# A fused attention, MLP and Fourier block on one core: TensorE's attention work grouped by two units, and two copies moved to other engines

## The chip, the cores and the metric

One core of a Trainium2 chip runs the whole program. The metric is the device time of one execution in microseconds (us); the median of three runs of the kernel before is 860.5 us (857.07 to 861.02).

TensorE is PE in the profile (PEld its weight loads), VectorE is DVE, ScalarE is ACT, GpSimd is POOL, and SyncE, which issues most DMAs, is SP.

## The reference

```python
def _attn_ref(q, k, v):                      # (2, 12, 448, 64) each, fp32
    scores = np.matmul(q, k.transpose(0, 1, 3, 2)) / np.sqrt(64)
    scores = np.where(mask_above_diagonal, -1e9, scores)
    attn = np.exp(scores - np.max(scores, axis=-1, keepdims=True))
    attn = attn / (np.sum(attn, axis=-1, keepdims=True) + 1e-09)
    return np.matmul(attn, v)
...
x = attention as (2, 448, 768)
x = x + relu(layernorm(x) * g_ln @ w_ch1) @ w_ch2          # 768 -> 3072 -> 768
u = x + real(fft2(x))
u = u + relu(layernorm(u) @ w2_ch1) @ w2_ch2
```

All of it is wanted at nearly fp32 precision. The kernel therefore splits most operands into a rounded part (type fp32r) and a rest, and multiplies three times.

## The kernel before, in words

**Stages.** Attention for 2 batches comes first (to about 107 us of the span), then the first MLP, the Fourier mix (from about 460 us), and the second MLP. In the MLPs PE is fed without a gap: line 95, 96 and 97 are the three products of a split matmul of 448 columns. The change touches the attention stage alone.

**Attention's units.** Heads are taken in pairs, 6 per batch, so 12 pairs. A pair has 448 rows of scores per head, cut into four *units*: u0 and u1 hold blocks 0 and 2 (128 rows each) of the first and of the second head, u2 holds block 1 of both heads, and u3 the last 64 rows of both heads, which share one block of 128 rows. There are 48 units, and the loop over `i` near the end of `fused_kernel` (lines 702 to 747 before) goes through them with each step shifted:

- `scores` (L282, PE): q times k into banks of PSUM named `sps`. Units u0 and u1 are done together. u3 uses `zd`, a padded copy of q.
- `row_max` (L299, DVE): adds the mask and takes the row minimum of the negated scores.
- `exps` (L311, ACT): the exponential into a tile `pexp`, with the row sum collected beside it.
- `transposes` (L355, PE): four 128x128 transposes into a bank `tps`, and `transposed` (L360, ACT), the copy of that bank to `pT`.
- `values` (L374, PE): v times `pT` into `avps`. Nothing is done at u0; the work for u0 and u1 is done at u1, then that of u2 and of u3. `avps` lies in a pool of one bank, so a pair's first value matmul waits until the pair before has been read out.

Seven banks of PSUM serve everything else in turn.

**Once for each pair.** `sum_recip` (L320 to L323, DVE) makes the reciprocals of the row sums. `spread` (L330, PE) transposes them to a few rows, which ACT copies to `divrow` (L334). `spread_rows` (L340 and L344, PE) spreads those rows over all partitions into a bank, and the bank is copied to `inv` (L349, ACT). `scaled` (L399, DVE) multiplies `avps` by `inv`, and `ln_sum` (L424, DVE) adds the result to a running sum for the layer norm. Where `pr >= HJ`, `moved` shifts the result by one partition with two DMAs that POOL issues (L410, L411).

**Operands.** `split_q` runs on POOL from the third pair on (L241 rounded part, L242 rest, L245 into `zd`). `split_k` makes k's rounded part on ACT (L253; for the very first pair on DVE, L251) and its rest on DVE (L254). Raw q, k, v and the raw weights share one pool of 6 buffers.

**What else runs in the attention stage.** From unit 32 on, the first MLP's weights are loaded, and from unit 38 on they are split in pieces (`w_tick`: L167 and L91 on ACT, L168, L170, L174 and L92 on DVE). After batch 0's last pair its layer norm starts (L438 on PE, L440 and L466 on ACT, L446 and L476 on DVE). The first MLP's first matmuls need only batch 0 and follow attention directly on PE.

**Order.** Each engine runs its instructions strictly in its own order. The program's order is a priority: a scheduler places every instruction on its engine from it, so an engine's final order is not the order of the source, and weight pieces land well ahead of the unit that asks for them.

Of the kernel before, what the change touches and what calls it, by code (L numbers as in the profile page):

```python
# [14 lines left out]
ACTF = mybir.ActivationFunctionType  # L15
# [4 lines left out]
B, H, S, D = 2, 12, 448, 64  # L20
# [4 lines left out]
PAIRS = [3, 4, 5, 0, 1, 2]  # L25
# [5 lines left out]
ES = 4  # L31
W_LOAD, W_FROM, W_EARLY = 32, 38, 6
SPLIT_AT = {1: (1, 1), 2: (2, 5)}
AHEAD, L_T, L_C, L_V = (3, 1, 2, 3)
Q_AT, K_AT = (0, 1)
NB1, NB2 = 3, 6
NJ = DM // P
HJ = NJ // 2
# [14 lines left out]
def fused_kernel(ctx: ExitStack, tc: tile.TileContext, aps, out):  # L53
    nc = tc.nc
# [149 lines left out]
    xa = {}  # L204
# [42 lines left out]
    def split_k(b, pr):  # L247
        k = kparts[b, pr] = t_tile([P, 2, S], "ks")
        src = q_raw[b, pr][:, 1]
        if (b, pr) == pairs[0]:  # L250
            yield nc.vector.tensor_scalar_mul(k[:, 0], src, -(D**-0.5))  # L251
        else:
            yield nc.scalar.activation(out=k[:, 0], in_=src, func=ACTF.Copy, scale=-(D**-0.5))  # L253
        yield nc.vector.scalar_tensor_tensor(  # L254
            out=k[:, 1], in0=src, scalar=-(D**-0.5), in1=f32(k[:, 0]), op0=ALU.mult, op1=ALU.subtract
        )
# [48 lines left out]
    def exps(i):  # L305
        b, pr, unit = units[i]
        e = exp_tiles[i % ES]
        flat = e.rearrange("p a b -> p (a b)")
        sp, st = s_ps.pop(i), stat[b, pr]
        for col, at, c, to, n in widths(unit):  # L310
            nc.scalar.activation(  # L311
                out=flat[:, to : to + n], in_=sp[at][:, c : c + n], func=ACTF.Exp, scale=-1.0, bias=st[:, 0, col : col + 1],
                accum_out=st[:, 1, col : col + 1],
            )
        p_sb[i] = e
# [20 lines left out]
    def spread_rows(b, pr):  # L336

        ps, rows = spread_ps.pop((b, pr)), diag.pop((b, pr))
        for t in range(3):
            nc.tensor.matmul(  # L340
                out=ps[:, t * P : (t + 1) * P], lhsT=pick[:, t], rhs=rows, start=True, stop=True, skip_group_check=True
            )
        for r in range(2):
            nc.tensor.matmul(  # L344
                out=ps[:, 3 * P : S], lhsT=pick[:, 3 + r], rhs=rows[:, own[r]], start=(r == 0), stop=(r == 1),
                skip_group_check=True,
            )
        inv[b, pr] = p_tile("inv")
        nc.scalar.activation(out=inv[b, pr], in_=ps[:, :S], func=ACTF.Copy)  # L349

    def transposes(i):
        e = p_sb.pop(i)
        tp = bank("tps")
        for a in range(4):
            nc.tensor.transpose(out=tp[:, a * P : (a + 1) * P], in_=e[:, a], identity=ident)  # L355
        t_ps[i] = tp

    def transposed(i):
        t = t_tile([P, 4, P], "pT", F32)
        nc.scalar.activation(  # L360
            out=t.rearrange("p a q -> p (a q)"), in_=t_ps.pop(i), func=ACTF.Copy
        )
        pT[i] = t
# [327 lines left out]
    scored = AHEAD  # L691
# [3 lines left out]
    def ln_first():  # L695
        now, *after = ln_rest(0, g_sb)
        bg.extend(now)
        late.append(after)

    later = {}  # L700
    i = 0
    while i < n + L_V or max(later, default=0) >= i:
        pi, at = divmod(i, per)
        if 0 <= i - L_T < n:
            transposes(i - L_T)
        while scored <= min(i + AHEAD, n - 1) and units[scored][:2] in kparts:
            scores(scored)
            scored += 1
        if i < n:
            red = row_max(i)  # L710
        if 0 <= i - L_C < n:
            transposed(i - L_C)
        for f in later.pop(i, []):
            f()
        if i == 0:
            exps(0)
        for f, p in splits.pop(i, []):
            for _ in f(*pairs[p]) or ():
                pass
        if at == 2 and pi + 3 < len(pairs):  # L720
            load_pair(*pairs[pi + 3])
        if i >= W_LOAD and n_raw[0] < n_split[0] + 2:
            w_load()
        if i >= W_FROM:
            w_tick(1, W_EARLY)
        with tc.issue_after(red.ins):
            bg_step()
        if 0 < i < n:
            exps(i)
        if 0 <= i - L_V < n:  # L730
            values(i - L_V)
            b, pr, _ = units[i - L_V]
            if (i - L_V) % per == per - 1:
                scaled(b, pr)
                ln_sum(b, pr, xa)
                if pr >= HJ:
                    later.setdefault(i + 1, []).append(lambda b=b, pr=pr: moved(b, pr))
                if (b, pr) == (0, PAIRS[-1]):
                    later.setdefault(i + 1, []).append(lambda: ln_first())
        if i < n and i % per == per - 1:  # L740
            b, pr, _ = units[i]
            later.setdefault(i + 1, []).append(lambda b=b, pr=pr: sum_recip(b, pr))
            later.setdefault(i + 2, []).append(lambda b=b, pr=pr: spread(b, pr))
            later.setdefault(i + 3, []).append(lambda b=b, pr=pr: spread_rows(b, pr))
        i += 1
    raw_ahead[0] = 2
    while bg:
# [145 lines left out]
```

## Time and profile before

| | before |
|---|---|
| runs, us | 857.07, 860.5, 861.02; median 860.5 |
| profiled execution, us | 857.58 |
| its span, us | 855.7 |
| PE busy | 841.3 us, 98% |
| DVE busy | 599.1 us, 70% |
| ACT busy | 331.9 us, 39% |
| POOL busy | 46.0 us, 5% |

Busy shares are averages over stages. In the timeline a row starts at the first number, and the second is the time until its last instruction ends; matmuls overlap, so what a block of matmuls costs on PE is the distance between the start of its row and the start of the next row. A bracket tells how long the engine was idle before the row and what ended that.

### The profile page before, as it was taken

Reading aid. Unit: us, or ns where it says so; the run is one execution under the profiler, and the core shown is the slowest. Engines: PE = TensorE matmul, PEld = TensorE weight load, DVE = VectorE, ACT = ScalarE, POOL = GpSimd, SP = SyncE. Lnnn points to the kernel's source line nnn. Section 1 sums busy time; section 2 is a strip of 40 time slices with the busy share of each in tenths; the row PEclk is TensorE's granted clock in tenths of the full one; section 3 lists DMA queues with packets and bytes.
Section 4 is the critical chain, followed back from the end, with each engine's and each line's share of the span. In section 5 each row is a group of like instructions: output and inputs, shape, how many; then the busy total and the mean of one; then the engine's idle time right before and its main releaser. Section 6 shows DMA issues by size and latency. Waiting matters only on the chain.

```text
span 855.7 us, 11863 instructions
## 1 busy us (share of the span) xinstructions
PE 841.3 (98%) x4664; PEld 756.6 (88%) x4664; DVE 599.1 (70%) x1019; ACT 331.9 (39%) x627; POOL 46.0 (5%) x91
## 2 busy tenths in 40 slices
PE   6999999999999999999999999999999999999997
PEld 5776789899999999999998889899999999999997
DVE  5789999796666566666699789696666566666432
ACT  6898975323332333223234245322332233223200
POOL 5433000100000000000101000000000000000000
PEclk9999999999999999999999999999999999999999
DMA  5434644333333333333615203324333332320011
GB/s 205 136 103 133 201 151 171 117 105 117 111 111 110 111 111 111 111 111 107 204 60 197 74 1 105 117 74 149 110 101 109 102 100 107 111 74 1 1 65 64
DMA packets 21431, 93.28 MB, mean 109 GB/s; under 512 B 2768, under 2 KB 4568, under 8 KB 21376
## 3 DMA queue, kind: packets, MB, share of 16 engines
q1 hardware_dynamic: 19152, 86.68, 29.9%
q0 software_dynamic: 2080, 5.62, 2.1%
q8 instruction: 36, 0.59, 0.3%
q10 hardware_dynamic: 144, 0.23, 0.1%
q14 instruction: 19, 0.16, 0.1%
HBM read 88.40 MB, written 2.75 MB: 107 GB/s over the span
## 4 chain that ended last, share of the span: by engine, by line
PE 93%; DVE 3%; ACT 2%; DMA 1%; issue 1%; DVEq 0%; ACTq 0%; SPq 0%
PE hps L97 14%; PE hps L96 14%; PE hps L95 14%; PE yps L95 14%; PE yps L97 14%; PE yps L96 14%; PE sps L282 2%; PE tps L355 2%; PE avps L374 2%; ACT pexp L311 1%; DVE sps L299 1%; PE mixps L95 1%; PE mixps L96 1%; PE mixps L97 1%; PE abps L95 1%
## 5 line engine op out<-in xcount | busy, mean ns | idle before, releaser
L95 PE MATMUL yps<-h,wsp 128*128 128x448 f32 x576 | 211.3, 367 | 0.0
L97 PE MATMUL hps<-xn,wsp 128*128 128x448 f32 x576 | 211.0, 366 | 0.0
L95 PE MATMUL hps<-xn,wsp 128*128 128x448 f32 x576 | 211.0, 366 | 0.0
L96 PE MATMUL yps<-h,wsp 128*128 128x448 f32 x576 | 210.7, 366 | 0.0
L96 PE MATMUL hps<-xn,wsp 128*128 128x448 f32 x576 | 210.6, 366 | 0.0
L97 PE MATMUL yps<-h,wsp 128*128 128x448 f32 x576 | 210.5, 365 | 0.0
L91 ACT ACTIVATE wsp<-wbits 128x768 fp32r<-128x768 f32 x96 | 80.9, 842 | 171.1 <-PE yps L97 159.2
L167 ACT ACTIVATE wbits<-wraw 128x768 f32<-128x768 f32 x96 | 86.3, 899 | 95.2 <-DVE wsp L92 94.5
L95 PEld LDWEIGHTS hps<-xn,wsp 128*128 128x128 f32 x576 | 108.2, 188 | 9.2 <-issue 0.4
L96 PEld LDWEIGHTS yps<-h,wsp 128*128 128x128 f32 x576 | 108.2, 188 | 9.1 <-issue 0.6
L97 PEld LDWEIGHTS hps<-xn,wsp 128*128 128x128 f32 x576 | 108.2, 188 | 9.1 <-issue 0.2
L96 PEld LDWEIGHTS hps<-xn,wsp 128*128 128x128 f32 x576 | 108.2, 188 | 9.0 <-issue 0.2
L95 PEld LDWEIGHTS yps<-h,wsp 128*128 128x128 f32 x576 | 108.2, 188 | 8.9 <-issue 0.4
L97 PEld LDWEIGHTS yps<-h,wsp 128*128 128x128 f32 x576 | 108.2, 188 | 8.8 <-issue 0.2
L517 ACT ACTIVATE h<-hps 128x448 fp32r<-128x448 f32 x96 | 52.2, 545 | 147.9 <-PE hps L97 147.7
L518 DVE SCALAR_TENSOR_TENSOR h<-hps,h 128x448 fp32r<-128x448 f32 x96 | 59.4, 621 | 69.3 <-ACT h L517 69.2
L539 DVE TENSOR_TENSOR x<-x,yps 128x448 f32<-128x448 f32 x96 | 58.9, 617 | 68.3 <-PE yps L97 68.2
L92 DVE TENSOR_TENSOR wsp<-wbits,wsp 128x768 fp32r<-128x768 f32 x96 | 91.9, 957 | 19.0 <-ACT wsp L91 14.2
L168 DVE TENSOR_SCALAR wbits<-wbits 128x768 uint32<-128x768 uint32 x96 | 53.5, 557 | 64.0 <-ACT wbits L167 63.4
L170 DVE SCALAR_TENSOR_TENSOR wbits<-wraw,wbits 128x768 uint32<-128x768 uint32 x96 | 91.8, 956 | 2.3
L174 DVE SCALAR_TENSOR_TENSOR wbits<-wraw,wbits 128x768 uint32<-128x768 uint32 x96 | 92.0, 959 | 0.4
L311 ACT ACTIVATE pexp<-sps,stat 128x128 f32<-128x128 f32 (+3 forms) x84 | 41.3, 506 | 8.3 <-DVE stat L299 7.6
(123 smaller groups left out, 644.8 us busy)
## 6 DMA issues: line engine op xcount, KB each, us to landing
wraw<-in_w SPq DMA_DIRECT2D x96, 768.0 KB, 4.2
qkv<-in_qk SPq DMA_DIRECT2D x11, 448.0 KB, 4.8
qkv<-in_v SPq DMA_DIRECT2D x12, 256.0 KB, 5.3
out_t<-x SPq DMA_DIRECT2D x12, 224.0 KB, 1.9
x<-xr POOLq DMA_DIRECT2D x6, 222.2 KB, 4.0
cd<-in_cd POOLq DMA_DIRECT2D x3, 386.0 KB, 4.0
sd<-in_sd POOLq DMA_DIRECT2D x3, 386.0 KB, 6.2
cs<-in_cs POOLq DMA_DIRECT2D x2, 448.0 KB, 5.0
```

The lines of the kernel that those rows point to most:

```text
L91: nc.scalar.activation(out=hi, in_=src, func=ACTF.Copy)
L92: nc.vector.tensor_tensor(out=lo, in0=src, in1=f32(hi), op=ALU.subtract)
L95: nc.tensor.matmul(out=dst, lhsT=w_lo, rhs=x_hi, start=first, stop=False)
L96: nc.tensor.matmul(out=dst, lhsT=w_hi, rhs=x_lo, start=False, stop=False)
L97: nc.tensor.matmul(out=dst, lhsT=w_hi, rhs=x_hi, start=False, stop=last)
L167: nc.scalar.activation(out=f, in_=high.bitcast(F32), func=ACTF.Copy, scale=EXPONENTS)
L168: nc.vector.tensor_scalar(out=bits, in0=bits, scalar1=3, scalar2=None, op0=ALU.logical_shift_left)
L170: nc.vector.scalar_tensor_tensor(out=bits, in0=high, scalar=0x80000000, in1=bits, op0=ALU.bitwise_and, op1=ALU.bitwise_or)
L174: nc.vector.scalar_tensor_tensor(out=bits, in0=low, scalar=29, in1=bits, op0=ALU.logical_shift_right, op1=ALU.bitwise_or)
L517: nc.scalar.activation(out=t[:, 0], in_=src, func=ACTF.Relu)
L518: nc.vector.scalar_tensor_tensor(out=t[:, 1], in0=src, scalar=0.0, in1=f32(t[:, 0]), op0=ALU.max, op1=ALU.subtract)
L539: nc.vector.tensor_tensor(out=xx, in0=xx, in1=y, op=ALU.add)
```

## The change

The loop now works on two units at a time on PE: at even `i` it issues the transposes of both units before, then the scores of the next two units, then the values of two units. The reciprocals of a pair are made at the first unit of the next pair, and `spread`, the scores, and `spread_rows` come at its third. k's rounded part is made by POOL from the second pair on. The bank with the spread reciprocals is copied by DVE.

```diff
-AHEAD, L_T, L_C, L_V = (3, 1, 2, 3)
+AHEAD = 4
...
-            yield nc.scalar.activation(out=k[:, 0], in_=src, func=ACTF.Copy, scale=-(D**-0.5))
+            yield nc.gpsimd.tensor_scalar_mul(k[:, 0], src, -(D**-0.5))
...
-        nc.scalar.activation(out=inv[b, pr], in_=ps[:, :S], func=ACTF.Copy)
+        nc.vector.tensor_copy(out=inv[b, pr], in_=ps[:, :S])
...
-    while i < n + L_V or max(later, default=0) >= i:
+    while i < n + 4 or max(later, default=0) >= i:
         pi, at = divmod(i, per)
-        if 0 <= i - L_T < n:
-            transposes(i - L_T)
-        while scored <= min(i + AHEAD, n - 1) and units[scored][:2] in kparts:
-            scores(scored)
-            scored += 1
+        done = pairs[pi - 1] if 0 < pi <= len(pairs) else None
+        if i % 2 == 0:
+            for u in (i - 2, i - 1):
+                if 0 <= u < n:
+                    transposes(u)
+            if at == 2 and done:
+                spread(*done)
+            while scored <= min(i + 3, n - 1) and units[scored][:2] in kparts:
+                scores(scored)
+                scored += 1
+            if at == 2 and done:
+                spread_rows(*done)
         if i < n:
             red = row_max(i)
-        if 0 <= i - L_C < n:
-            transposed(i - L_C)
+        if i % 2 == 0 and i < n:
+            exps(i)
+        if 0 <= i - 2 < n:
+            transposed(i - 2)
         for f in later.pop(i, []):
             f()
-        if i == 0:
-            exps(0)
...
-        if 0 < i < n:
+        if i % 2 and i < n:
             exps(i)
-        if 0 <= i - L_V < n:
-            values(i - L_V)
-            b, pr, _ = units[i - L_V]
-            if (i - L_V) % per == per - 1:
-                scaled(b, pr)
-                ln_sum(b, pr, xa)
...
+        if at == 0 and done:
+            sum_recip(*done)
+        if i % 2 == 0:
+            for u in (i - 4, i - 3):
+                if 0 <= u < n:
+                    values(u)
+        if at == 2 and done:
+            b, pr = done
+            scaled(b, pr)
+            ln_sum(b, pr, xa)
...
-        if i < n and i % per == per - 1:
-            b, pr, _ = units[i]
-            later.setdefault(i + 1, []).append(lambda b=b, pr=pr: sum_recip(b, pr))
-            later.setdefault(i + 2, []).append(lambda b=b, pr=pr: spread(b, pr))
-            later.setdefault(i + 3, []).append(lambda b=b, pr=pr: spread_rows(b, pr))
         i += 1
```

What this does to the engines' order shows at three places.

**PE, one pair of the steady stage, before** (from the scores of u0 and u1; the values of u0 and u1 and the transposes of u1 follow):

```order
L282 MATMUL sps<-ks,qs 128x128 x6
L282 MATMUL sps<-ks,qs 128x384 x6
L330 MATMUL invps<-ident,div 14x128
L374 MATMUL avps<-pT,qkv 64x128 x4
L355 MATMUL tps<-ident,pexp 128x128 x4
L340 MATMUL invps<-divrow,pick 128x128 x3
L344 MATMUL invps<-divrow,pick 128x64 x2
L374 MATMUL avps<-pT,qkv 64x64 x8
L355 MATMUL tps<-ident,pexp 128x128 x4
L282 MATMUL sps<-ks,qs 128x256 x6
L355 MATMUL tps<-ident,pexp 128x128 x4
L282 MATMUL sps<-ks,zd_89 128x448 x3
```

And of the change:

```order
L355 MATMUL tps<-ident,pexp 128x128 x8
L330 MATMUL invps<-ident,div 14x128
L282 MATMUL sps<-ks,qs 128x128 x6
L282 MATMUL sps<-ks,qs 128x384 x6
L340 MATMUL invps<-divrow,pick 128x128 x3
L344 MATMUL invps<-divrow,pick 128x64 x2
L374 MATMUL avps<-pT,qkv 64x128 x4
L374 MATMUL avps<-pT,qkv 64x64 x8
L355 MATMUL tps<-ident,pexp 128x128 x8
L282 MATMUL sps<-ks,qs 128x256 x6
L282 MATMUL sps<-ks,zd_89 128x448 x3
L374 MATMUL avps<-pT,qkv 64x128 x8
```

Four blocks of transposes have become two, and the values of u2 and u3 stand together. The instructions are the same.

**DVE, in the second pair** (the row maxima of u2, of width 256, and of u3, of width 448, beside the rests of k for the third and fourth pair), before:

```order
L322 CAST div<-stat 128x7
L299 ISA sps,stat<-sps,maskw 128x256
L299 ISA stat 128x1
L323 TENSOR_TENSOR div<-stat,div 128x7
L299 ISA sps,stat<-sps,maskw 128x256
L299 ISA stat 128x1
L299 ISA sps,stat<-sps,maskf 128x448
L299 ISA stat 128x1
L254 SCALAR_TENSOR_TENSOR ks<-qkv,ks 128x448 x2
L320 TENSOR_SCALAR stat<-stat 128x7
```

And of the change:

```order
L322 CAST div<-stat 128x7
L299 ISA sps,stat<-sps,maskw 128x256
L299 ISA stat 128x1
L323 TENSOR_TENSOR div<-stat,div 128x7
L254 SCALAR_TENSOR_TENSOR ks<-qkv,ks 128x448 x2
L299 ISA sps,stat<-sps,maskw 128x256
L299 ISA stat 128x1
L299 ISA sps,stat<-sps,maskf 128x448
L299 ISA stat 128x1
L320 TENSOR_SCALAR stat<-stat 128x7
```

The two rests of k stand ahead of the last row maxima of the pair, where they stood behind them. On ACT, at the same place, the copy to `divrow` now stands behind the exponential of u3, where it stood ahead of it.

**DVE, at the end of attention** (from the split of a weight tile behind the last row maximum to the last pair's L323), before:

```order
L92 TENSOR_TENSOR wsp<-wbits,wsp 128x768
L168 TENSOR_SCALAR wbits<-wbits 128x768
L170 SCALAR_TENSOR_TENSOR wbits<-wraw,wbits 128x768
L399 TENSOR_TENSOR x<-avps,inv 128x448
L320 TENSOR_SCALAR stat<-stat 128x7
L174 SCALAR_TENSOR_TENSOR wbits<-wraw,wbits 128x768
L424 TENSOR_TENSOR lnacc<-lnacc,x 128x448
L321 RECIPROCAL stat<-stat 128x7
L168 TENSOR_SCALAR wbits<-wbits 128x768
L322 CAST div<-stat 128x7
L170 SCALAR_TENSOR_TENSOR wbits<-wraw,wbits 128x768
L323 TENSOR_TENSOR div<-stat,div 128x7
```

And of the change:

```order
L92 TENSOR_TENSOR wsp<-wbits,wsp 128x768
L320 TENSOR_SCALAR stat<-stat 128x7
L168 TENSOR_SCALAR wbits<-wbits 128x768
L321 RECIPROCAL stat<-stat 128x7
L170 SCALAR_TENSOR_TENSOR wbits<-wraw,wbits 128x768
L349 COPY inv<-invps 128x448
L322 CAST div<-stat 128x7
L174 SCALAR_TENSOR_TENSOR wbits<-wraw,wbits 128x768
L399 TENSOR_TENSOR x<-avps,inv 128x448
L323 TENSOR_TENSOR div<-stat,div 128x7
```

The product L399 of the pair before the last, which frees the bank `avps`, has moved to the end of this piece, just ahead of the last L323, and the copy L349 has come in ahead of it.

## Rows read from the trace of the kernel before

**Rows 1.** The page, busy time and share of the span of each engine:

```profile
PE 841.3 (98%) x4664; PEld 756.6 (88%) x4664; DVE 599.1 (70%) x1019; ACT 331.9 (39%) x627; POOL 46.0 (5%) x91
```

**Rows 2.** Busy time by stage: PE, PEld, DVE, ACT, POOL, PE's granted clock, DMA:

```profile
78.50:81.80 3.30, 3.30 (x23) 2.63 (x18) 3.30 (x12) 2.70 (x8) 0.00 (x0) 0.50 0.61 184
90.00:100.00 10.00, 9.22 (x102) 7.01 (x102) 10.00 (x31) 9.91 (x30) 1.02 (x2) 1.00 0.59 187
```

**Rows 3.** Timeline of PE, one pair of the steady stage:

```profile
48.39 0.66 PE L355 MATMUL tps<-ident,pexp 128*128 128x128 f32 x4
48.98 1.12 PE L282 MATMUL sps<-ks,qs 64*128 64x128 f32 x12
...
50.24 0.66 PE L374 MATMUL avps<-pT,qkv 128*64 128x128 f32 x8
50.83 0.66 PE L355 MATMUL tps<-ident,pexp 128*128 128x128 f32 x4
...
53.84 0.66 PE L355 MATMUL tps<-ident,pexp 128*128 128x128 f32 x4
54.25 0.85 PE L282 MATMUL sps<-ks,zd 128*128 128x448 f32 x3
55.03 1.09 PE L374 MATMUL avps<-pT,qkv 128*64 128x128 f32 x16
56.05 0.66 PE L355 MATMUL tps<-ident,pexp 128*128 128x128 f32 x4
```

**Rows 4.** Timeline of all engines, the second pair:

```profile
15.64 1.14 POOL L242 TENSOR_TENSOR qs<-qkv,qs 128x448 fp32r<-128x448 f32 x1
...
15.84 0.96 DVE L322 CAST div<-stat 128x7 fp32r<-128x7 f32 x1
...
16.84 0.62 POOL L245 CAST zd<-qs 64x128 fp32r<-64x128 f32 x2
...
19.45 1.16 DVE L254 SCALAR_TENSOR_TENSOR ks<-qkv,ks 128x448 fp32r<-128x448 f32 x2 [1.25 <-ACT ks L253]
...
21.93 0.17 DVE L322 CAST div<-stat 128x7 fp32r<-128x7 f32 x1
...
29.09 0.69 PE L374 MATMUL avps<-pT,qkv 128*64 128x64 f32 x16
```

**Rows 5.** Instructions by line and form, 0 to 130 us (busy us, mean ns):

```profile
L170 DVE SCALAR_TENSOR_TENSOR wbits<-wraw,wbits 128x768 uint32<-128x768 uint32 x8 | 7.6, 955 | 0.1
...
L349 ACT ACTIVATE inv<-invps 128x448 f32<-128x448 f32 x12 | 6.4, 531 | 0.1
...
L253 ACT ACTIVATE ks<-qkv 128x448 fp32r<-128x448 f32 x11 | 6.1, 560 | 0.0
...
L241 POOL CAST qs<-qkv 128x448 fp32r<-128x448 f32 x10 | 5.6, 558 | 0.8 <-DMA qkv<-in_qk 0.3
...
L168 DVE TENSOR_SCALAR wbits<-wbits 128x768 uint32<-128x768 uint32 x8 | 4.4, 549 | 1.0 <-ACT wbits L167 0.7
...
L399 DVE TENSOR_TENSOR x<-avps,inv 128x448 f32<-128x448 f32 x6 | 3.7, 622 | 1.0 <-ACT inv L349 0.9
```

**Rows 6.** Timeline of all engines, where the first weights come in:

```profile
60.59 0.62 DVE L399 TENSOR_TENSOR x<-avps,inv 128x448 f32<-128x448 f32 x1 [0.61 <-ACT inv L349]
...
65.12 0.90 ACT L167 ACTIVATE wbits<-wraw 128x768 f32<-128x768 f32 x1 [0.64 <-DMA wraw<-in_w]
```

**Rows 7.** Timeline of all engines, PE's longest wait in attention:

```profile
75.68 0.52 DVE L320 TENSOR_SCALAR stat<-stat 128x7 f32<-128x7 f32 x1 [1.21 <-ACT pexp L311]
...
76.47 0.95 DVE L322 CAST div<-stat 128x7 fp32r<-128x7 f32 x1
...
77.33 0.55 PE L340 MATMUL invps<-divrow,pick 14*128 14x128 f32 x3 [1.71 <-ACT divrow L334]
```

**Rows 8.** Timeline of all engines, attention's end and the MLP's start on PE:

```profile
106.88 0.16 DVE L323 TENSOR_TENSOR div<-stat,div 128x7 fp32r<-128x7 f32 x1
107.09 0.28 PE L330 MATMUL invps<-ident,div 128*14 128x128 f32 x1 [0.76 <-DVE div L323]
...
108.46 0.47 PE L97 MATMUL hps<-xn,wsp 128*128 128x448 f32 x1
```

More of the change, by code (lines that the diff above doesn't have):

```diff
@@ L727, in fused_kernel @@
             bg_step()
-        if 0 < i < n:
+        if i % 2 and i < n:
             exps(i)
-        if 0 <= i - L_V < n:
-            values(i - L_V)
-            b, pr, _ = units[i - L_V]
-            if (i - L_V) % per == per - 1:
-                scaled(b, pr)
-                ln_sum(b, pr, xa)
[L736 to L739, printed above, removed]
-        if i < n and i % per == per - 1:
-            b, pr, _ = units[i]
-            later.setdefault(i + 1, []).append(lambda b=b, pr=pr: sum_recip(b, pr))
-            later.setdefault(i + 2, []).append(lambda b=b, pr=pr: spread(b, pr))
-            later.setdefault(i + 3, []).append(lambda b=b, pr=pr: spread_rows(b, pr))
+        if at == 0 and done:
[8 more added lines that the diff above has]
+            ln_sum(b, pr, xa)
+            if pr >= HJ:
+                later.setdefault(i + 1, []).append(lambda b=b, pr=pr: moved(b, pr))
+            if (b, pr) == (0, PAIRS[-1]):
+                later.setdefault(i + 1, []).append(lambda: ln_first())
         i += 1
```

## The prediction

> **What bounds the kernel now.** I read the page first: PE is busy for 98% of the span [rows 1], so whatever shortens the time must let PE's MLP work begin earlier. From 108 us on PE runs one matmul of 448 columns after another without a gap, so the question is only when attention lets go of PE. Then I read the stages. In the steady stage of attention PE's timeline shows no idle time at all and a pair takes from 48.39 to 56.05, 7.66 us [rows 3]: PE is the bound there, for the four pairs from about 29 to 60 us. From 66 us on, when weight pieces and the layer norm are added, DVE is the bound: between 90 and 100 us it is busy 10.00 of 10 us, while PE is down to 9.22 [rows 2]. ACT, at 9.91, is close behind. Attention ends on the chain L323 on DVE, L330 on PE, and PE takes up the MLP for good at 108.46, with two of its matmuls already done [rows 8], so in effect at 108.1.
>
> **The change, part by part.** I follow the shift of PE's work against the profiled execution.
>
> *The start of attention (first two pairs): +0.8 us.* On ACT two k copies go, 0.56 us each [rows 5]. But in DVE's new order the rests of k for the third and fourth pair stand ahead of the last row maxima of the second pair, and the fourth pair's k comes late from POOL. POOL's L242 ends at 16.78 [rows 4]; behind it stand one k, two casts into zd (0.62, rows 4) and the next k. POOL has no row of a product with a number; the nearest are its one-input cast at 0.56 [rows 5] and its two-input op at 1.14 [rows 4]. I take 0.56, the same number of inputs, and keep 1.14 for the range. That ends at about 18.7; a rest is half of 1.16 us [rows 4], so the maxima end near 20.2. Before, they were done when DVE's wait of 1.25 us began, at 18.2 [rows 4]. Two us late, less 1.1 that ACT saved: +0.9, and I take +0.8, from 29.09 to 29.9 for the value matmuls of that pair's last unit [rows 4]. With k at 1.14, +2.0; if ACT's saving covers the delay, -0.2.
>
> *The four PE-bound pairs: -1.2 us.* Sixteen passes of values cost 1.02 us (55.03 to 56.05) and eight cost 0.59 (50.24 to 50.83) [rows 3]: eight passes are 0.43, and beginning another kind of block costs 0.16. Before, a pair has three transpose blocks of 0.59 and one of 0.41 (53.84 to 54.25, in front of a full-size block) [rows 3], 2.18 in all; two blocks of eight at 0.59 plus 0.43 are 2.04. Values of u2 and u3 in one block save another 0.16. So 0.30 a pair. At the least, if only the transposes gain, 0.14; at most, if L330 now also costs no new beginning behind transposes, 0.46: -0.6 to -1.8.
>
> *Where batch 0's layer norm begins, at about 60 us: +0.4 us.* On PE five value matmuls of the next pair now stand directly behind the last values of a pair. They need its one bank `avps` read out by L399, 0.62 us and now behind the copy of `inv` [rows 6]; before, scores of u2 lay between. Zero if later work gives it back, +1.0 with L399 and two handovers.
>
> *The DVE-bound stretch, 66.0 (end of the first L167, rows 6) to the last L323's end at 107.0 [rows 8]: -1.9 us.* I counted DVE's rows between these marks in both orders. The change adds five copies of `inv`, which I price like the other op that reads a bank of 448 columns, L399, at 0.62 [rows 5], so +3.1. A rest of k, a layer-norm sum, an L168 and an L170 fall out of the stretch (0.58, about 0.6, 0.55 and 0.96; rows 4 and 5), -2.7. So work is nearly even, +0.4. What goes is waiting: 1.21 us for an exponential [rows 7], which was late on ACT; two pairs later in that queue ACT is lighter by 2 x (0.53 + 0.56) = 2.2 us [rows 5], more than that. And two tiny ops that took 0.52 and 0.95 us there [rows 7], where one such takes 0.17 [rows 4], lost 1.1; both ran beside POOL's queue, which now lies otherwise. I count both as gone, and keep for the range that they stay or that a third comes. Bounds -2.3 and +1.0.
>
> *The end: +2.2 us.* Before, PE needs from L323's end at 107.04 to 108.1, that is 1.0. In the new order L399 of the last pair but one ends only with L323, so the last pair's values all come after it: 1.02 for u0 and u1, then L330 to the end of the spread, 1.37 (107.09 to 108.46, rows 8), with 0.4 of the values of u2 and u3 (0.59 and 0.6 less 0.16, rows 3 and 4) covering the wait for `divrow` as two MLP matmuls do now, and 0.15 for handovers: 3.2. If the scheduler's order is kinder in time, +1.0.
>
> The moved copy of k costs ACT nothing and DVE nothing directly; POOL has idle time in every pair. `sum_recip` moves by half an iteration in source only: on DVE it keeps its place behind u3's maximum. SP's loads keep their order and hang on the same last values of a pair. A loop turn more (n + 4) issues nothing new.
>
> Sum: 0.8 - 1.2 + 0.4 - 1.9 + 2.2 = +0.3. The profiled execution took 857.58, so 857.9. The runs shown lie at 857.07, 860.5 and 861.02; with the profiled one their mean is 859.0, 1.4 above it, and the median of a few runs may fall on either side. I add 0.6, a little under half: **858.5 us**, no change that can be told from 860.5. About 0.5% (4.3 us) is what a measurement of this kernel can tell from no change.
>
> **The rivals.**
>
> *ACT was the bound behind DVE (faster).* Both waits in rows 7 name ACT, and it is busy 9.91 of 10 [rows 2]. If each of the last five pairs is a ring of DVE, ACT and PE with ACT as its slow link, taking 1.09 us of ACT's work out of each gives -5.5 instead of -1.9, and the start gives -0.2 instead of +0.8: -4.3 in all, 853.9 with the same 0.6. Against it: DVE has no idle time between 90 and 100 us, and the copy goes to DVE of all engines.
>
> *The row copy becomes PE's wait (slower).* On ACT `divrow` now stands behind the exponential of u3, and PE's L340 stands 2.3 us behind the start of eight transposes: 1.02 for these and 1.26 for L330 and the scores of u0 and u1 (48.98 to 50.24, rows 3). If that exponential ends later than 1.8 us after this start, PE waits in every pair, as once before for 1.71 us [rows 7]. After that wait PE's granted clock was half (0.50, that is 1.2 GHz, from 78.5 to 81.8, rows 2), with 3.3 us of busy time at half speed. At 0.8 us a pair the four pairs cost +2.0 instead of -1.2, and two such stretches up to 1.6 each: +6.7 in all, 864.9. Against it: ACT loses 1.09 us of work a pair, and following one steady pair by hand through the new order with these durations I find the exponential done about 1.0 us after the start.
>
> *POOL holds DVE (a little slower).* While POOL's L242 ran, DVE's L322 took 0.96 us instead of 0.17 [rows 4]. Eleven new POOL ops give eleven new chances, of which four (two at the start, two behind 66 us) lie where DVE is waited for: 4 x 0.56 is +2.2, and with k at 1.14 another +1.2: +3.7 in all, 861.9. The Trainium skill, GPSIMD Engine Reference, section 8 (Key points), says that POOL shares its SBUF interfaces with VectorE and contends with DVE instructions in a 2-port mode or with two SBUF inputs; the two rows agree, and by that rule more of DVE's ops are open to it than the tiny ones. The same page, section 3.1, gives a best case of 1.8 cycles an element for a tight loop, by which k would take an estimated 0.67 us at 1.2 GHz; the start would then come to about +1.0.
>
> That the change does not do what it says is excluded: the order shows the blocks, the copies and their engines.
>
> **How the numbers follow.** The forecast has 0.55 (its own range 856 to 861), ACT as bound 0.20, POOL's holds 0.13, the row copy 0.12. The range of 853.5 to 862.5 holds the first three and leaves out the far part of the last. Faster than 856.2 takes half to two thirds of the second case and a tenth of the first: 0.20. Slower than 864.8 is most of the last case and a little of the third: 0.10. The rest, 0.70, is no change.
>
> **What would show it.** In the steady stage a pair should take 7.3 to 7.4 us, with no wait on L340; the value matmuls of the second pair's u3 should begin near 29.9; PE should wait before the five value matmuls at about 60 us; the 1.71 us wait and the half clock behind it should be gone; DVE should have no idle time from 66 us to the last L323, near 105, and the MLP should then start some 3 us behind it, near 108. A time under 855 would mean that ACT held the last pairs, one over 863 that L340 waits in each.

## The result, and the profile after

The kernel before took 858.86 us in the median of four runs (857.07 to 861.02), the changed one 869.0 (868.89 to 869.85): a ratio of 1.0123, 95% interval 1.0101 to 1.0146. The change makes the kernel slower by some 10 us. The prediction was 858.5 with a range to 862.5, and no change as the likeliest case; it was wrong. The kernel before has runs near 857 and runs near 860 us in changing shares, so experiments are compared by their ratios and not by their medians, and of e2's four runs two, at 927 and 1038 us with a granted clock of 0.85 and 0.75, do not count.

The page of the changed kernel, busy time by engine, against [rows 1]:

```profile
PE 842.3 (97%) x4664; PEld 760.0 (88%) x4664; DVE 606.7 (70%) x1031; ACT 323.4 (37%) x604; POOL 63.3 (7%) x102
```

Work only moved: 8.5 us left ACT, 7.6 went to DVE, 17.3 to POOL, PE has 1.0 more. So 10 us of waiting must be new. The times of the last value matmul (L374) of each pair tell where. In this table, read from the two timelines, the last column is the first L97, the third of the MLP's matmuls. (The two profiled executions, of 857.58 and 868.89 us, lie 11.3 apart.)

| us | pair 2 | pair 6 | pair 7 | pair 8 | pair 9 | pair 10 | L97 |
|---|---|---|---|---|---|---|---|
| before | 29.77 | 60.43 | 69.12 | 78.79 | 87.85 | 96.02 | 108.46 |
| after | 34.53 | 65.91 | 75.91 | 83.90 | 96.14 | 105.19 | 119.38 |
| later by | 4.76 | 5.48 | 6.79 | 5.11 | 8.29 | 9.17 | 10.92 |

Nearly 5 us are lost by the second pair, under 1 in the four pairs that follow, and 5.4 from there to the end. Now the stages of the changed kernel, against [rows 2] (us; PE, PEld, DVE, ACT, POOL busy; granted clock; DMA share; GB/s):

```profile
21.10:27.80 6.70, 4.41 (x35) 4.23 (x36) 4.63 (x19) 4.47 (x16) 0.25 (x1) 0.50 0.05 11
82.00:89.00 7.00, 3.85 (x46) 3.17 (x45) 6.61 (x15) 3.09 (x9) 3.42 (x5) 1.00 0.36 115
90.00:100.00 10.00, 9.34 (x97) 7.70 (x97) 8.78 (x29) 8.31 (x24) 3.84 (x6) 0.86 0.35 114
```

Two stretches stand out: PE's granted clock is half from 21.1 to 27.8 us, and from 82 to 89 us PE works 3.85 of 7.

**The start.** Rows of POOL, DVE and ACT from their timelines, in order of time; they answer to [rows 4]:

```profile
16.79 1.32 POOL L253 TENSOR_SCALAR ks<-qkv 128x448 fp32r<-128x448 f32 x1
18.07 0.92 POOL L245 CAST zd<-qs 64x128 fp32r<-64x128 f32 x2
18.15 0.69 DVE L254 SCALAR_TENSOR_TENSOR ks<-qkv,ks 128x448 fp32r<-128x448 f32 x1 [1.31 <-POOL ks L253]
19.08 1.33 POOL L253 TENSOR_SCALAR ks<-qkv 128x448 fp32r<-128x448 f32 x1
20.44 0.95 DVE L254 SCALAR_TENSOR_TENSOR ks<-qkv,ks 128x448 fp32r<-128x448 f32 x1 [1.60 <-POOL ks L253]
21.65 0.66 DVE L299 CUSTOM_DVE_ANT_0 sps<-sps,maskf 128x448 f32<-128x448 f32 x1
21.88 0.47 ACT L311 ACTIVATE pexp<-sps,stat 128x256 f32<-128x256 f32 x1 [4.23 <-DVE stat L299]
23.09 0.25 ACT L334 ACTIVATE divrow<-invps 14x128 fp32r<-14x128 f32 x1
```

And PE's timeline:

```profile
23.39 0.90 PE L340 MATMUL invps<-divrow,pick 14*128 14x128 f32 x3 [3.59 <-ACT divrow L334]
24.09 0.57 PE L344 MATMUL invps<-divrow,pick 14*128 14x64 f32 x2
24.59 1.98 PE L374 MATMUL avps<-pT,qkv 128*64 128x128 f32 x24
26.50 1.74 PE L355 MATMUL tps<-ident,pexp 128*128 128x128 f32 x8
```

Read it as one chain. POOL takes 1.32 us for k's product. DVE stands still twice for it, 1.31 and 1.60 us, and the row maxima of u2 and u3 of the second pair stand behind these two rests of k. So the maxima end at 22.3 us where the prediction had 20.2, ACT idles 4.23 us, `divrow` comes at 23.09 (on ACT it is behind u3's exponential), and PE stands 3.59 us. During that wait the granted clock fell to half, and the next blocks ran at half speed: 24 passes of values took 1.91 us (24.59 to 26.50), while the same block takes 1.05 in a later pair (48.27 to 49.32, below).

**The steady pairs.** PE's timeline of the changed kernel, against [rows 3]:

```profile
41.78 1.09 PE L355 MATMUL tps<-ident,pexp 128*128 128x128 f32 x8
...
48.27 1.12 PE L374 MATMUL avps<-pT,qkv 128*64 128x128 f32 x24
49.32 0.88 PE L355 MATMUL tps<-ident,pexp 128*128 128x128 f32 x6
...
51.98 0.85 PE L282 MATMUL sps<-ks,zd 128*128 128x448 f32 x3 [1.01 <-POOL ks L253]
...
56.79 0.55 PE L340 MATMUL invps<-divrow,pick 14*128 14x128 f32 x3 [0.74 <-ACT divrow L334]
```

From the second pair's last value to the third's it is 7.32 us (34.53 to 41.85) instead of 7.66. But the pair from 49.39 to 58.58 takes 9.19, with the two waits shown in it. The first bracket names POOL's k, but that k is for a later pair and ends at 51.98, while PE's weight loads for these scores already begin at 51.95. What ended just ahead was ACT's exponential of u0, at 51.84; it was late because DVE's row maxima were, and these stand behind a wait of 1.90 us for k (L254 at 47.99). The second wait comes by way of the row maximum of u3: ahead of it a rest of k took 1.48 us on DVE (at 53.74; the median is 0.69) while POOL worked on q and k. The rows of POOL and DVE for an earlier pair of this stage show why k is late:

```profile
35.06 0.62 DVE L399 TENSOR_TENSOR xr<-avps,inv 128x448 f32<-128x448 f32 x1
35.99 0.62 POOL L410 DMA_DIRECT2D x<-xr  x1 [3.31 <-DVE xr L399]
36.61 0.51 POOL L411 DMA_DIRECT2D x<-xr  x1
37.13 1.15 POOL L242 TENSOR_TENSOR qs<-qkv,qs 128x448 fp32r<-128x448 f32 x1
38.25 1.33 POOL L253 TENSOR_SCALAR ks<-qkv 128x448 fp32r<-128x448 f32 x1
39.62 0.70 DVE L254 SCALAR_TENSOR_TENSOR ks<-qkv,ks 128x448 fp32r<-128x448 f32 x1 [1.86 <-POOL ks L253]
40.24 0.26 DVE L320 TENSOR_SCALAR stat<-stat 128x7 f32<-128x7 f32 x1
```

POOL's 3.31 us of idle time before L410 are no spare time: its queue stands behind a DMA issue that waits for the result of the pair before on DVE. Only then come the second DMA issue, q's rest and k's product, 3.6 us in all (35.99 to 39.58), and DVE waits 1.86 us for the last of them ahead of the reciprocals.

**From 66 us on.** The timeline of all engines, around PE's second long wait:

```profile
79.77 1.36 DVE L446 TENSOR_TENSOR xc<-xr,mean 128x448 f32<-128x448 f32 x1
...
80.54 1.78 POOL L253 TENSOR_SCALAR ks<-qkv 128x448 fp32r<-128x448 f32 x1
...
82.35 0.70 DVE L254 SCALAR_TENSOR_TENSOR ks<-qkv,ks 128x448 fp32r<-128x448 f32 x1 [1.22 <-POOL ks L253]
...
83.91 1.73 POOL L242 TENSOR_TENSOR qs<-qkv,qs 128x448 fp32r<-128x448 f32 x1
...
84.56 1.49 DVE L168 TENSOR_SCALAR wbits<-wbits 128x768 uint32<-128x768 uint32 x1
...
86.08 0.96 DVE L170 SCALAR_TENSOR_TENSOR wbits<-wraw,wbits 128x768 uint32<-128x768 uint32 x1
...
87.97 0.62 DVE L349 COPY inv<-invps 128x448 f32<-128x448 f32 x1
88.20 0.37 ACT L311 ACTIVATE pexp<-sps,stat 128x128 f32<-128x128 f32 x1 [3.79 <-DVE stat L299]
...
88.73 0.98 PE L282 MATMUL sps<-ks,zd 128*128 128x448 f32 x3 [3.06 <-DVE inv L349]
```

DVE waits for POOL, then works off weight pieces (one L168 takes 1.49 us while POOL's L242 runs; the mean of 96 is 0.57), then the maxima, and only at 87.97 copies the spread reciprocals out of their bank. PE needs that bank for the scores of u3 and stands 3.06 us; the granted clock is half again behind this wait, for 3.4 us.

Where batch 0's layer norm begins, and at attention's end, PE's timeline and one row of DVE's, against [rows 6] and [rows 8]:

```profile
67.40 0.84 PE L374 MATMUL avps<-pT,qkv 128*64 128x128 f32 x10 [1.50 <-ACT pexp L311]
...
115.37 0.16 DVE L323 TENSOR_TENSOR div<-stat,div 128x7 fp32r<-128x7 f32 x1
115.56 1.09 PE L374 MATMUL avps<-pT,qkv 128*64 128x128 f32 x16 [1.43 <-ACT pT L360]
...
118.87 0.47 PE L95 MATMUL hps<-xn,wsp 128*128 128x448 f32 x1
```

At 67.40 the exponentials that these values need had long been done; the next pair's first values wait for the one bank `avps`, which L399 reads out until 67.30. At 115.56 it is the same: the `pT` named was done at 114.82, and L399 reads `avps` until 115.46. At the end the MLP begins 3.3 us behind L323's end (115.53 to 118.87).

By form, the two operations of k and the moved copy, over the whole span (busy us, mean ns | idle time of the engine before them):

```profile
L253 POOL TENSOR_SCALAR ks<-qkv 128x448 fp32r<-128x448 f32 x11 | 15.7, 1430 | 2.0 <-DMA qkv<-in_qk 1.8
L254 DVE SCALAR_TENSOR_TENSOR ks<-qkv,ks 128x448 fp32r<-128x448 f32 x12 | 9.0, 752 | 9.6 <-POOL ks L253 9.5
L349 DVE COPY inv<-invps 128x448 f32<-128x448 f32 x12 | 7.4, 620 | 0.0
```

On ACT the rounded part took 560 ns, the copy 531 [rows 5]. DVE now idles 9.5 us for POOL.

### The profile page after: what moved, and what is told of

It reads as the page before. It is cut to its first block, busy times and chain, and to the rows that moved or that the text cites. A ratio compares the mean times of both kernels' runs of the same rounds, so it can differ in the third digit from the quotient of the medians.

```text
span 867.2 us, 11877 instructions
## 1 busy us (share of the span) xinstructions
PE 842.3 (97%) x4664; PEld 760.0 (88%) x4664; DVE 606.7 (70%) x1031; ACT 323.4 (37%) x604; POOL 63.3 (7%) x102
## 4 chain that ended last, share of the span: by engine, by line
PE 86%; DVE 1%; ACT 1%; issue 0%; ACTq 0%
PE hps L95 14%; PE hps L97 14%; PE hps L96 14%; PE yps L95 14%; PE yps L97 13%; PE yps L96 13%; PE mixps L95 1%; PE mixps L96 1%; PE mixps L97 1%; PE abps L95 1%; PE abps L96 0%; PE abps L97 0%; DVE sps L299 0%; PE rps L492 0%; PE lnv L459 0%; PE avps L374 0%
## 5 line engine op out<-in xcount | busy, mean ns | idle before, releaser
L97 PE MATMUL hps<-xn,wsp 128*128 128x448 f32 x576 | 211.1, 366 | 0.0
L97 PE MATMUL yps<-h,wsp 128*128 128x448 f32 x576 | 210.5, 365 | 0.0
L97 PEld LDWEIGHTS hps<-xn,wsp 128*128 128x128 f32 x576 | 108.2, 188 | 9.2 <-issue 0.2
L97 PEld LDWEIGHTS yps<-h,wsp 128*128 128x128 f32 x576 | 108.2, 188 | 8.8 <-issue 0.2
L168 DVE TENSOR_SCALAR wbits<-wbits 128x768 uint32<-128x768 uint32 x96 | 54.6, 569 | 63.1 <-ACT wbits L167 62.7
```

The lines of the kernel that those rows point to most:

```text
L97: nc.tensor.matmul(out=dst, lhsT=w_hi, rhs=x_hi, start=False, stop=last)
L168: nc.vector.tensor_scalar(out=bits, in0=bits, scalar1=3, scalar2=None, op0=ALU.logical_shift_left)
```

## The experiments

All ratios are to the kernel before, run on the same chip beside each kernel, with a 95% interval. "Waits for k" is DVE's idle time ahead of L254 put down to k's rounded part, "half clock" how long PE's granted clock was half between 15 and 125 us of the span; both are of the profiled run.

| | order | k made by | `inv` by | ratio | waits for k, us | half clock, us |
|---|---|---|---|---|---|---|
| the change | grouped | POOL, product | DVE | 1.0123 | 9.5 | 10.2 |
| e1 | grouped | ACT | DVE | 1.0025 | 0 | 6.8 |
| e2 | grouped | POOL, product | ACT | 1.0100 | 8.7 | 13.7 |
| e3 | grouped | ACT | ACT | 1.0024 | 2.1 | 6.8 |
| e4 | before | POOL, product | ACT | 1.0018 | 1.0 | 6.8 |
| e5 | grouped | POOL, cast | DVE | 1.0063 | 3.8 | 6.8 |
| e6 | grouped, rest of k later | POOL, product | DVE | 1.0053 | 7.4 | 13.7 |
| e7 | grouped | POOL, cast | ACT | 1.0008 | 2.6 | 10.2 |
| e8 | before | POOL, product | DVE | 1.0009 | 0 | 3.4 |
| e9 | grouped, rest of k later | POOL, cast | DVE | 0.9990 | 3.6 | 0 |
| e10 | first six pairs grouped | ACT | ACT | 0.9991 | 1.8 | 3.4 |
| e11 | last six pairs grouped | ACT | ACT | 1.0021 | 1.3 | 6.8 |
| e12 | first six pairs grouped | POOL, cast | ACT | 1.0013 | 2.5 | 3.4 |
| e13 | grouped, rest of k later | POOL, product | ACT | 1.0046 | 7.2 | 6.8 |
| e14 | first six grouped, rest of k later | POOL, cast | DVE | 0.9999 | 2.7 | 0 |

### Which part of the change costs: e1 to e4

e1 takes the change and gives k's rounded part back to ACT:

```diff
-            yield nc.gpsimd.tensor_scalar_mul(k[:, 0], src, -(D**-0.5))
+            yield nc.scalar.activation(out=k[:, 0], in_=src, func=ACTF.Copy, scale=-(D**-0.5))
```

> The change with k's rounded part back on ACT; the grouping and DVE's copy of inv stay. Theory POOL: the product on POOL, 1.43 us where I had put 0.56, keeps DVE's rests of k, and the row maxima behind them, waiting (9.5 us in all), so this run loses the 3.6 us wait at L340 near 23 us and takes 860 to 863 us, 6 to 9 under the change. Theory bank: DVE's late copy of inv is most of the loss, so this run stays at 866 to 869. Theory grouping: the pairwise order is itself most of it; also 866 to 869.

Measured: 860.77 us, ratio 1.0025 [1.0003, 1.0047], as theory POOL had it. This one line holds about 8 of the 10 us. The wait at L340 at the start is gone.

e2 gives back the copy instead:

```diff
-        nc.vector.tensor_copy(out=inv[b, pr], in_=ps[:, :S])
+        nc.scalar.activation(out=inv[b, pr], in_=ps[:, :S], func=ACTF.Copy)
```

> The change with the copy of inv back on ACT; k stays on POOL. Theory bank: the 3.1 us wait of the scores of u3 near 88 us and the half clock behind it go, and 863 to 866 us are left. Theory POOL: DVE waits for k as before and the time falls by 2 us at most, 867 to 869. Theory grouping: 867 to 869.

Measured: 866.37 and 866.49 us, ratio 1.010 [1.0062, 1.0137], between the two theories. PE's wait of 3.59 us at the start is still there. The scores of u3 near 88 us wait 1.83 us instead of 3.06, and in e1 they wait 1.35: both moves have a part in that wait. By the times the copy's share is 2.6 us, but the interval holds the change's own ratio.

e3 has both lines back, the grouping alone.

> The grouping alone, both copies on ACT as before the change. Theory POOL and theory bank, which add up: no loss is left, and with 0.3 us gained in each PE-bound pair it takes 855 to 860 us, like the kernel before or a little under. Theory grouping: 864 us or more.

Measured: 860.84, ratio 1.0024 [1.0007, 1.0042], a little above the 855 to 860 that was expected and the same as e1: with k on ACT no cost of the copy on DVE can be told.

e4 is the reverse: the kernel before, with k on POOL alone (the diff of e1 with its signs exchanged).

> The kernel before with k's rounded part on POOL and nothing else changed. Theory POOL: DVE's rests of k wait for POOL here too; 862 to 867 us, with waits of DVE L254 for POOL of over 4 us in all. Theory bank or grouping: 858 to 861, since ACT loses 6 us of work and k is not late.

Measured: 860.15, ratio 1.0018 [1.0001, 1.0036], not the 862 to 867 of theory POOL:

```profile
L253 POOL TENSOR_SCALAR ks<-qkv 128x448 fp32r<-128x448 f32 x11 | 15.0, 1368 | 1.4 <-DMA qkv<-in_qk 0.6
L254 DVE SCALAR_TENSOR_TENSOR ks<-qkv,ks 128x448 fp32r<-128x448 f32 x12 | 9.8, 816 | 1.1 <-POOL ks L253 1.0
```

POOL's product is nearly as long here, but DVE waits 1.0 us for it instead of 9.5. So neither move nor the grouping is dear by itself: k on POOL costs 8 us only where the grouped order asks for it early.

### Length or place: e5, e6, e9

e5 shortens POOL's operation: a plain cast, with the factor -1/8 moved into the row maxima and their mask. Lines from L254 on are two lower in the kernels with this edit (maxima L297, scores of u3 L280, copy L347).

```diff
...
-            yield nc.gpsimd.tensor_scalar_mul(k[:, 0], src, -(D**-0.5))
-        yield nc.vector.scalar_tensor_tensor(
-            out=k[:, 1], in0=src, scalar=-(D**-0.5), in1=f32(k[:, 0]), op0=ALU.mult, op1=ALU.subtract
-        )
+            yield nc.gpsimd.tensor_copy(out=k[:, 0], in_=src)
+        yield nc.vector.tensor_tensor(out=k[:, 1], in0=src, in1=f32(k[:, 0]), op=ALU.subtract)
...
-                out=o, in0=o, in1=mask[:, mask.shape[1] - n :], scale=1.0, scalar=1e38, op0=ALU.add, op1=ALU.min,
+                out=o, in0=o, in1=mask[:, mask.shape[1] - n :], scale=-(D**-0.5), scalar=1e38, op0=ALU.add, op1=ALU.min,
```

> The change, with POOL making k's rounded part as a plain copy (one input, no factor; POOL's casts of the same tile took 0.56 us in the kernel before), the factor -1/8 being applied by the row maxima instead; the rest of k is then a two-input subtract on VectorE at the same place. Theory 1 (the LENGTH of POOL's 1.43 us product is what the grouped order cannot hide): POOL's operation falls under 0.7 us, VectorE's waits for ks fall from 9.5 us to under 3 us, and the time goes back to 859 to 862. Theory 2 (it is that ANY work on POOL for k stands behind q's part and the zd casts, whatever its length, or that VectorE's own copy of the spread 1/row-sum is the cost): the time stays at 866 to 869. If the product's 1.43 us comes from sharing with VectorE and not from the factor, POOL's copy takes 1.1 to 1.4 us too and the time lies at 866 to 869.

Measured: 863.65, ratio 1.0063 [1.0036, 1.0090], between the two forecasts. The groups by form:

```profile
L253 POOL CAST ks<-qkv 128x448 fp32r<-128x448 f32 x11 | 7.0, 633 | 0.6 <-DMA qkv<-in_qk 0.5
L254 DVE TENSOR_TENSOR ks<-qkv,ks 128x448 fp32r<-128x448 f32 x12 | 8.3, 688 | 3.8 <-POOL ks L253 3.8
```

Without the factor POOL's operation on the same tile takes 0.63 us in the mean instead of 1.43. About half the loss goes with it, not all. PE's two long waits shrink and stay: the scores of u3 wait 2.32 us at 84.24, and at the start it is, in PE's timeline of e5:

```profile
21.90 0.55 PE L338 MATMUL invps<-divrow,pick 14*128 14x128 f32 x3 [2.52 <-ACT divrow L332]
```

e6 leaves POOL's product as it is and issues the rest of k three units later, for the fourth and later pairs; on DVE it then stands behind row maxima that it stood ahead of.

```diff
-            for _ in f(*pairs[p]) or ():
+            steps = f(*pairs[p])
+            if steps is not None and p >= 3:
+                next(steps)
+                later.setdefault(i + 3, []).append(lambda steps=steps: next(steps))
+                continue
+            for _ in steps or ():
```

> The change, with the rest of k of the fourth and later pairs issued three units later, which puts it on VectorE behind row maxima that it stood ahead of; POOL's product is as long as in the change. Theory 1 (the cost is VectorE held by POOL at a place ahead of row maxima that ScalarE and TensorE wait for): VectorE's waits for ks fall below 6 us and the time lies at 861 to 866; Theory 2 (POOL itself is late for the scores, wherever the rest stands): the scores wait instead, and the time stays at 867 to 872.

Measured: 863.81, ratio 1.0053 [1.0037, 1.0070]. The time is as theory 1 had it, but the waits for k only fell to 7.4 us, not under 6. It is not their sum that counts but what stands behind them: PE's two long waits, 3.59 and 3.06 us in the change, are 1.05 and 0.78 in e6's timeline.

```profile
20.95 0.84 PE L340 MATMUL invps<-divrow,pick 14*128 14x128 f32 x3 [1.05 <-ACT divrow L334]
...
84.11 0.85 PE L282 MATMUL sps<-ks,zd 128*128 128x448 f32 x3 [0.78 <-ACT pexp L311]
```

e9 has both edits.

> e5_short_k and e6_rest_later together: POOL makes k's rounded part as a plain copy, and the rest of k of the fourth and later pairs is issued three units later; the spread 1/row-sum stays on VectorE as in the change. Theory 1 (what the change lost is VectorE standing still for POOL's k ahead of row maxima, by length and by place): the waits for ks fall under 2 us, and the time joins the runs with k on ScalarE, 860 to 861.5. Theory 2 (the copy of the spread 1/row-sum on VectorE has a price of its own of 2 to 3 us beside POOL's k): the time stays at 863 to 864, where each of the two stood alone.

Measured: 859.18, a little under the 860 to 861.5 of theory 1, ratio 0.9990 [0.9978, 1.0003]. The whole loss is gone, with k on POOL and the copy on DVE as in the change. e5 takes off 0.60%, e6 0.70%, together 1.30%, and e9 took off 1.33%: as far as the intervals (some 0.1 to 0.3% to either side) can tell, length and place add up. Its groups by form, and its stages:

```profile
L254 DVE TENSOR_TENSOR ks<-qkv,ks 128x448 fp32r<-128x448 f32 x12 | 7.8, 651 | 3.7 <-POOL ks L253 3.6
L280 PE MATMUL sps<-ks,zd 128*128 128x448 f32 x36 | 11.6, 434 | 0.3 <-DVE inv L347 0.3
```

```profile
21.10:27.80 6.70, 6.70 (x80) 5.55 (x81) 4.49 (x18) 5.44 (x18) 2.54 (x4) 1.00 0.44 141
82.00:89.00 7.00, 6.90 (x77) 5.57 (x73) 7.00 (x26) 5.17 (x17) 1.34 (x4) 1.00 0.26 71
```

The waits for k did not fall under 2 us as expected; 3.6 are left. But the scores of u3 now wait 0.3 us for the copy instead of 3.6, and the granted clock is not half anywhere. The waits that are left stand where nobody waits behind them: this one, in DVE's timeline, is followed by the reciprocals, and no pair on PE is longer for it (second to sixth pair end at 31.09, 38.41, 45.72, 53.03, 60.35).

```profile
35.51 0.68 DVE L254 TENSOR_TENSOR ks<-qkv,ks 128x448 fp32r<-128x448 f32 x1 [1.04 <-POOL ks L253]
```

One caution on the start: in the profile of e9 PE's first blocks run slowly for longer, though the granted clock reads 1.00 there as in the changed kernel. Eight transposes take 1.89 us there at 14.63 (to 16.52), while at 13.10 four take 0.65 in the changed kernel:

```profile
13.10 0.65 PE L355 MATMUL tps<-ident,pexp 128*128 128x128 f32 x4
```

```profile
14.63 1.97 PE L353 MATMUL tps<-ident,pexp 128*128 128x128 f32 x8
```

With PE later, POOL's k is less late for it, and the start of e9 has no wait at all; part of what its first two pairs show may be that. The profiles of e1, e3, e8 and e12 to e14 begin as late. That of e4 begins as early as the changed kernel's, and PE does not wait at L340 in its start. The eleven runs of e9 lie within 857.37 to 859.65, so its total doesn't hang on this one profile.

### The copy on DVE: e7, e8, e13

e7 is e5 with the copy of `inv` on ACT, e13 is e6 with it, e8 is the kernel before with both copies moved; the lines are those of e1 and e2.

> As e5_short_k, with the spread 1/row-sum copied by ScalarE as before the change. If the copy on VectorE is harmless once VectorE no longer waits for POOL (the two runs with k on ScalarE lie at 860.77 and 860.84), this is within 1 us of e5_short_k. If VectorE's copy costs by itself, this is 2 to 3 us faster than e5_short_k, as the change with only that copy moved back was (866.4 against 869.0).

> The kernel before with both copies moved (k's rounded part on POOL, the spread 1/row-sum on VectorE) and its order of units kept. Theory 1 (the cost is an interaction with the grouped order): 859.5 to 861.5, VectorE's waits for ks under 3 us. Theory 2 (the two moves cost by themselves, order or no order): 864 to 869.

> e6_rest_later with the spread 1/row-sum copied by ScalarE as before the change. If VectorE's copy, standing behind the waits for POOL that are left, is what e6 still loses: 860 to 861.5. If the loss left in e6 is the length of POOL's product by itself: 863 to 864.5. Both in part: 861.5 to 863.

Measured: e7 860.29, ratio 1.0008 [0.9995, 1.0021]; e8 860.16, ratio 1.0009 [0.9998, 1.0020]; e13 860.76, ratio 1.0046 [1.0031, 1.0061]. From e5 to e7 the copy is worth 0.55%, so it does cost where DVE still waits for POOL ahead of it. From e6 to e13 the ratios give 0.07%, the medians 3 us, since the kernel before had a median of 857.2 beside e13 and of 859.56 beside e6: how the rest of e6's loss divides stays open. e8 bears theory 1 out: with the order of before both moves together cost 0.2% at most, and DVE never waits for k:

```profile
L254 DVE SCALAR_TENSOR_TENSOR ks<-qkv,ks 128x448 fp32r<-128x448 f32 x12 | 8.4, 711 | 0.0
```

### The grouping itself: e10 to e12, e14

Here a condition on the pair decides between the two orders (`two = pi < 6`, in e11 `pi >= 6`), and each of the loop's steps is taken as the one or the other order has it.

```diff
-        if i % 2 == 0:
+        two = pi < 6
+        if not two or i % 2 == 0:
...
-        if i % 2 and i < n:
+        if (i % 2 or not two) and 0 < i < n:
             exps(i)
```

> Both copies on ScalarE as before; TensorE's work goes two units at a time in the first six pairs, and from the seventh pair on in the order of before. Theory 1 (the grouping gains 0.30 to 0.35 us for each pair bound by TensorE, and the loss of grouping alone, 1 us in all, comes from the pairs bound by VectorE): 858.0 to 859.0. Theory 2 (the gain per pair is given back at the start and where the order is left, because ScalarE and VectorE get their work in lumps): 859.6 to 861.0.

> The reverse of e10: the first six pairs in the order of before, the last six two units at a time, both copies on ScalarE. Theory 1 of e10 (the pairs bound by VectorE lose by the grouping, the prediction gave them a gain of 1.9 us): 861.0 to 862.5. Theory 2: 859.0 to 860.5. The prediction's step for this stretch would give 857.7.

> e10 with POOL making k's rounded part as a plain copy (the factor -1/8 in the row maxima), the spread 1/row-sum on ScalarE. Theory 1: as e10 or up to 1 us faster (857.0 to 859.0), ScalarE having 0.59 us less to do for each pair; if POOL's copy, on VectorE's path, costs what ScalarE gains, 859 to 860.

> The first six pairs two units at a time and the rest in the order of before, with POOL's plain copy of k, the rest of k three units later, and the spread 1/row-sum on VectorE. If the place of the rest of k is what made e12 slower than e10: 856.5 to 858.5, as e10 or faster. If POOL's share in k costs by itself in the order of before: 859.5 to 861.

Measured: e10 857.92, ratio 0.9991 [0.9975, 1.0006]; e11 861.63, ratio 1.0021 [1.0006, 1.0035]; e12 860.69, ratio 1.0013 [0.9997, 1.0029]; e14 857.56, ratio 0.9999 [0.9987, 1.0012]. The times of e10 and e11 are those of theory 1: the grouping is at best a small gain in the pairs bound by PE and a loss of 0.2% in those bound by DVE, where e11's PE waits 1.61 us ahead of scores and runs at half clock for 6.8 us behind that. e10's interval also holds 1, so its gain isn't shown. e12 missed (857.0 to 860 was expected, 860.69 came). e14, with the rest of k later and the copy on DVE, has the median that was expected of it if the place of the rest was the cause, but the kernel before had a median of 857.2 beside e14 and of 859.62 beside e12, and the intervals of their ratios overlap: this stays open. Beside the kernel before, neither e14 nor e9 nor e10 is a gain that can be told from none.

## Why the prediction was wrong

**The start (+0.8 forecast, 4.76 measured): the step that failed first.** The mechanism was in the text: k late from POOL, two rests of k ahead of the last row maxima of the second pair. Its price was not. "I take 0.56, the same number of inputs, and keep 1.14 for the range": the product took 1.32 there and 1.43 in the mean, above both ends, longer than the op with two inputs. The way of the delay to PE was wrong too. The 1.1 us that ACT saved were taken off it, but ACT idles 4.23 us for these maxima, so its saving is worth nothing here. The delay goes on through `divrow` to PE as a wait of 3.59 us, and the half clock that came with it adds about 2.2 (4.41 us of busy time at half speed between 21.1 and 27.8). e5 shows that the price was about half of it: with k near the price that was forecast (0.63 measured) PE still waits 2.52 us at this place, the second pair ends at 32.50, 2.7 later than before and not 0.8, and the kernel loses 0.63%.

**"The moved copy of k costs ACT nothing and DVE nothing directly; POOL has idle time in every pair": the second step that failed**, and the one that holds the place. What counts is not how long POOL idles but when k is ready and when DVE asks for it. Where a DMA issue that waits for DVE's L399 stands ahead of k in POOL's queue, k comes late (3.9 us behind L399's end, 35.68 to 39.58), and DVE, which is at its rest of k 2.1 us behind L399, stands still: 6.6 of the 9.5 us of waits are of this kind, the other 2.9 lie at the start. In e8, in the old order, k comes 3.5 us behind L399's end (25.77 to 29.28), behind the same two issues, but DVE is at the rest only at 30.72 and does not wait. e6 moved only the place and took off 0.7%; e4 shows the same POOL work in the old order with 1.0 us of waits. No run moves the issues themselves, so their share is not shown.

**The four PE-bound pairs (-1.2).** Right in size where nothing waits: 7.32 us for a pair instead of 7.66, that is -0.34 where -0.30 was forecast; e9 has all four at 7.31 to 7.32. In the changed kernel one of the four held the two new waits, and the four together came to +0.7.

**Batch 0's layer norm and the end (+0.4 and +2.2): right in kind.** The five values at 67.40 (ten passes in the row) wait 1.50 us for `avps`, and the pair loses 1.3, more than the +0.4 forecast and its upper bound of +1.0; the end takes 3.3 us from L323 to the MLP where 3.2 was forecast and 1.0 before.

**The DVE-bound stretch (-1.9 forecast): the third step that failed.** From the sixth pair's end to the MLP 5.3 us are lost (10.77 for the MLP's effective start, 108.1 to 118.87, less 5.48); without 1.3 and 2.3 for the two terms above, +1.7 are left for this one. It took it that DVE's waits go. The one behind PE's wait of 1.71 us did go, and the eighth pair won back 1.7 us (6.79 to 5.11 in the table). But others came: twice 1.22 us for k, at 82.35 and 93.49. And the copy of `inv`, counted as 0.62 us of work a pair, was also the release of a bank that PE waits for; the wait of 3.06 us behind it, with half a clock after it, was in no term.

e9, without these, reaches its first L97 at 108.72, 0.26 later than before. That this is near the sum's +0.3 is luck and bears nothing out: its second pair ends 1.3 later than before, behind the late start, and its rest of k stands at another place than the prediction had it. The kernel nearest to the one that was reckoned with, with k at 0.63 us in the place of the change, is e5, and it loses 0.63%.

**The rivals.** "POOL holds DVE" was nearest in its cause, at 861.9: it named POOL, but priced ops on DVE that run longer beside POOL (which are there: L168 1.49, L254 1.48), not DVE's waits for POOL's result. No rival reached 869.0. "The row copy becomes PE's wait" named L340 and the half clock, as they came at the start, but for another reason: the exponential was late because the maxima were, not because ACT was full. ACT as the bound is excluded by e8: both copies taken off ACT in the order of before gained nothing (1.0009 [0.9998, 1.0020]). Of the signs named ahead, the pair's 7.3 came; the time is over 863, but L340 waits once for 3.59 us and three times for 0.45 to 0.74, not in every pair, as that sign had it.

The Trainium skill, GPSIMD Engine Reference, section 4.1 (Engine selection), calls POOL's operations with one input "roughly line-rate". The cast comes near that (0.56 us for 448 columns, where DVE's own cast of such a tile takes 0.39 in e5); the product by a number, also with one input, does not, at 1.32 to 1.78 us, where DVE takes 0.39 for it (L251 in the kernel before). By the best case in section 3.1 of that page of the Trainium skill, 1.8 cycles an element, the prediction had an estimate of 0.67 us; the measured product is twice that.

## What to carry to other kernels

Before an operation moves to another engine, measure that very form there, by its operation and not by its count of inputs, or bound it well above the nearest rows. Then ask when the new engine can begin it (what stands ahead in its queue, and what that waits for) and what stands behind the consumer in the order of the new kernel: the same 1.4 us of POOL cost about 1.5 us in one order (e4) and 8 in the other. And count an operation that empties a bank not by its duration alone but by who waits for the bank.

## What the runs showed that was not expected

- On POOL a product by a number (128x448, fp32 to fp32r) takes 1.33 us while DVE stands idle and up to 1.78 beside DVE's L446, which itself took 1.36 instead of 0.62; the cast takes 0.56 and the two-input subtract 1.14.
- The granted clock went to half with PE's waits of about 3 us in both places of the changed kernel (from 21.0 and 89.3 us), but not with one of 1.50 us at 67.4; in the kernel before 1.71 us had been enough [rows 7], in e6 1.05 us (from 21.0) and in e4 1.00 us (from 62.3). The length of the wait alone doesn't tell.
- How long PE's first blocks run slowly at the start of attention differs between profiled runs, to about 10.8 us in the changed kernel's and 18.6 in e9's, at a granted clock of 1.00 in both, and a late start of full speed can hide a late operand.
